# A third pair of q-k products added on VectorE, background steps counted by their pitch, late softmaxes kept in PSUM, and a later load of T2

## The chip, the cores and the metric

The kernel runs on one core of one Trainium2 chip. The metric is the device time of one launch in microseconds (us); 715.28 is the median of three runs before the change.

## The reference

```python
x = A_x                                               # (1, 2048, 1024) bf16
g = _sigmoid((x * gate_w).sum(-1, keepdims=True))
# A: local attention, 32 heads of 32, 8 keys at distances 0, 2, ..., 14 behind the query
qkv = (x @ wqkv).reshape(B, S, 3, H, Dh) ...
logits = jnp.einsum("bhsd,bhswd->bhsw", q, kg) * Dh ** -0.5
logits = jnp.where(mask[None, None, :, :], logits, -1e9)
attn = _softmax(logits, axis=-1)
a = einsum("bhsw,bhswd->bhsd", attn, vg) ... @ wo
# B: gated MLP, Dm = 1024, Df = 3584
b = (_gelu(x @ w_gate) * (x @ w_up)) @ w_down
out = g * a + (1 - g) * b
```

## The kernel before

All large products are done by a seven-product scheme for 2 x 2 blocks: sums and differences of blocks ("forms") are made by VectorE, seven products by TensorE, and the results are put together in PSUM by copies and additions.

**The loop of units.** `units` lists 78 units: a pair of MLP columns, 16 units of q and k (eight for each half `s` of the sequence), eight of v, then the other MLP pairs, a gate and an up unit each. Iteration `b` is called a slot here. In each slot TensorE does, in this order, p1 of unit b (4 matmuls), p73 of unit b-1 (8), p5 of unit b (4), p2 and p6 of unit b (8), p4 of unit b-1 (4): 28 matmuls of 512 columns, all on line 355. The addition at the end of p73 (L401) is VectorE's: it reads the banks Y and Z, and p4 writes Y again. ScalarE copies banks (L377, L382, L390) and evacuates results (L361, L363, L409).

**Background tasks.** What VectorE does besides L401 comes from generators that stand in `tasks`, ordered by a priority. `run_bg(b, period)` is called once at the end of each slot: the credit is at most 0.3 left over plus the period (4.7 us in q, k and v, 4.8 after), and while it is over 0.3, the first task that is awake does a step and its price, a number that the step yields, is taken off. All of this happens while the program is recorded; on the chip the order is fixed. `Task.finish()` does all remaining steps of a task at once. The tasks that matter here:

- `sums_pair` (L315): four sums of weights for each MLP pair.
- `h_task` (L246, for the last pairs also L249): h = gelu(gate) * up, then a store to `h_d` on POOL's DMA queue (L252).
- `qk_prods` (L603 for two tiles at a time, L596 for one): the products q * k for 8 keys and three blocks of 256 positions each; each tile of 2048 columns stands in one of six buffers `prod`. `reduce_mm` on TensorE (L608) sums over head dimensions into banks 5 to 7: 12 matmuls for the products of one unit. For the units in `ADDED`, `qk_add` (L641) first adds the products of two units, and one reduction serves both.
- `spill` (L603, L596, L679 to L686): the same for the fourth block of each half, from q and k stored before.
- `softmax` and `softmax_back`: maximum (L713), subtraction (L715), exponential on ScalarE (L723), sum (L730), reciprocal, gate, product (L735), and a store to `w_d`. `softmax(a, cnt, ...)` does `cnt` blocks from block `a` on; number `e` says which of five it is. The exponent's argument and result stand in the arena (SBUF), at `R_EX[e]`.
- `pv_all` (L772 multiplies, L778 folds): attention times v for eight blocks, four tiles at a time, then a store to `o_d` (L796).
- `t_forms` (L895, L898), forms of the output weights, stored to `t_d`.

**The seam.** `run_last` follows the loop. It does p73 and p4 of the last unit, starts `down(0)`, queues the loads of T1 and T2 on SP's DMA queue and finishes all tasks. `pre_down_2` and `pre_down_3`, called when PV is done, have loaded most of the operands A12, A21, A22 and R21 (L838, L840, L857, on SP); `pre_down_4` queues the last parts of the four A operands on POOL's queue (L838): these come from `h_d` and wait for the last pair's first h store. `down(s)` then computes the output rows of half `s`: products of 512 columns (L1104) and, in `level2`, of 256 columns (L1071, seven products of 18 matmuls a group), with forms by VectorE: L943 scales, L952 combines, `forms_L` (L1029) and `forms_R` (L1037).

Of the kernel before, what the change touches and what calls it, by code (L numbers as in the profile page):

```python
# [15 lines left out]
P = 128  # L16
SC = 512
# [19 lines left out]
R_EX = (194.5, 81, 50, 81, 84)  # L37
R_MD = 72
R_ATTN = 73
# [3 lines left out]
R_PROD = 84  # L43
# [25 lines left out]
def kernel(  # L69
# [68 lines left out]
    with tc.manual_schedule(engines={mybir.EngineType.PE, mybir.EngineType.DVE, mybir.EngineType.Activation,  # L138
# [145 lines left out]
        def gate_task(s):  # L284
            ts = slice(s * SUP, (s + 1) * SUP)
            zc = small.tile([P, HK, ZI], F32, tag="zc", bufs=2)
            zs = small.tile([P, ZI], F32, tag="zs", bufs=2)
            go = small.tile([P, 2, ZI], BF16, tag="go", bufs=2)
            yield None
            nc.gpsimd.dma_start(out=zc[:], in_=z_d[:, ts].rearrange("g (p i) -> p g i", i=ZI))  # L290
            yield None
            V.tensor_reduce(out=zs[:], in_=zc[:].rearrange("p g i -> p i g"), axis=AX.X, op=ALU.add)
            nc.scalar.activation(out=zs[:], in_=zs[:], func=ACT.Tanh, scale=0.5)
            yield 0.15
            yield None
# [12 lines left out]
            gated.add(s)  # L308

        def sums_pair(w, sm):  # L310
            L11, L12 = w[:, :, 0:HK, 0:P], w[:, :, HK:KT, 0:P]
            L21, L22 = w[:, :, 0:HK, P:2 * P], w[:, :, HK:KT, P:2 * P]
            for o_, a, b_, op in ((sm[:, 0], L21, L22, ALU.add), (sm[:, 1], sm[:, 0], L11, ALU.subtract),
                                  (sm[:, 2], L11, L21, ALU.subtract), (sm[:, 3], L12, sm[:, 1], ALU.subtract)):
                TT(out=o_, in0=a, in1=b_, op=op)  # L315
                yield 0.64
# [97 lines left out]
        now = [0]  # L414

        class Task:
# [11 lines left out]
            def finish(self):  # L428
                while not self.done:
                    self.step()  # L430
# [7 lines left out]
        credit = [0.0]  # L438
# [54 lines left out]
        def h_task(G, U, i, s):  # L493
            h_store(G, U, i, s)
            yield 1.14 if i < NSC else 2.3

        def add_gu(w, sm, i, s):
            ug = add_unit(gu_forms(w, sm, 0), xf[s], "gate", st_tile)
            uu = add_unit(gu_forms(w, sm, 1), xf[s], "up", st_tile)
            uu.fin = lambda: bg(h_task(ug.T, uu.T, i, s), *((5.5, now[0]) if (i, s) == (NPAIR - 1, 0) else (7.5 if i == NPAIR - 1 else 0, now[0] + 1)))  # L500
# [74 lines left out]
        pr_off = [R_PR, R_PR + 4, R_PROD, R_PR + 8, R_PR + 12, R_PROD + 4]  # L575
# [19 lines left out]
        def qk_mult(dst, q, k):  # L595
            TT(out=dst, in0=q.rearrange("p (o s) -> p o s", o=1).to_broadcast([P, NWIN, AC]),  # L596
               in1=_win_ap(k, [[-DIL, NWIN], [1, AC]]), op=ALU.mult)

# [3 lines left out]
        def qk_mult2(dst, q, k, sq, sk):  # L602
            TT(out=dst, in0=_win_ap(q, [[sq, 2], [0, NWIN], [1, AC]]),  # L603
               in1=_win_ap(k, [[sk, 2], [-DIL, NWIN], [1, AC]]), op=ALU.mult)
# [7 lines left out]
        ADDED = {(1, 1), (1, 7)}  # L612
# [3 lines left out]
        def qk_prods(u, s, t):  # L616
# [21 lines left out]
        def qk_add(s, t):  # L638
            for a, b in ((0, 3), (2, 5)):
                u, v = ((pair_at(pr_off[i], pr_off[i + 1]) if a == 0 else reg(pr_off[i], NWIN * AC)) for i in (a, b))  # L640
                TT(out=u, in0=u, in1=v, op=ALU.add)  # L641
                yield 2.21 if a == 0 else 1.14
# [18 lines left out]
        SPILL = ((((R_PR, R_PR + 4), (R_PR + 8, R_PR + 12)), ((R_PR + 8, R_PR + 12), (R_PROD, R_PROD + 4))),  # L661
                 (((R_PROD, R_PROD + 4), (R_PR + 4, R_PR + 12)), ((R_PR + 4, R_PR + 12), (R_PR, R_PR + 8))))

        def spill(s):
# [3 lines left out]
            for g, (x, y) in enumerate(SPILL[s]):  # L668
                for i, ef in enumerate((x, y)):
                    t = QG * g + 2 * i  # L670
                    if credit[0] > 1.5:
                        qk_mult2(pair_at(*ef), qb[s][:, t, :], kb[s][:, t, HALO:HALO + AC], AC, KV)
                        yield 2.21
                        continue
                    for j in range(2):
                        qk_mult(reg3(ef[j], NWIN, AC), qb[s][:, t + j, :], kb[s][:, t + j, HALO:HALO + AC])
# [24 lines left out]
        def softmax(a, cnt, b0, e):  # L701
            ee = regf(R_EX[e], cnt * SC)
            e4 = ee.rearrange("p (a w s) -> p a w s", a=cnt, w=NWIN)
            sw = ee.rearrange("p (a w s) -> p a s w", a=cnt, w=NWIN)
            lg = banks[:, b0:b0 + cnt, :]
# [8 lines left out]
            yield 0.55 * cnt + 0.05  # L714
            TT(out=e4, in0=src, in1=bc(m), op=ALU.subtract)  # L715
            yield 0.55 * cnt + 0.05
# [5 lines left out]
        def softmax_exp(a, cnt, ee, e4, sw, m, bc):  # L722
            nc.scalar.activation(out=ee, in_=ee, func=ACT.Exp, scale=scale)  # L723
            bg(softmax_back(a, cnt, ee, e4, sw, m, bc), 3, now[0] + 1)

        def softmax_back(a, cnt, ee, e4, sw, m, bc):
# [7 lines left out]
            yield 0.65 * cnt  # L734
            TT(out=attn_all[:, a:a + cnt, :].rearrange("p a (w s) -> p a w s", w=NWIN), in0=e4, in1=bc(d), op=ALU.mult)  # L735
            yield 0.55 * cnt + 0.05
# [17 lines left out]
        def pv_all():  # L754
# [5 lines left out]
            for i, a in enumerate(PVO):  # L760
# [19 lines left out]
                for t in range(0, NT, 4):  # L780
                    if i + 1 == NBLK and t == 4:
                        load_A(Bs(0)["A12"], 0, 1, 0, 0, KX, False)
                    for step, n_ in ((lambda u, m: mult(u, m), 2), (lambda u, m: fold(u, m, 4), 4)):
                        u = t
                        while u < t + 4:
# [4 lines left out]
                            yield 2.21 if m == n_ else 1.14  # L790
                    fold(t, 4, 2)
                    yield 1.14
# [27 lines left out]
        at(Q0 + 2 * NT, lambda: [sv_task.step() for _ in range(2 - sv_n[0])])  # L820
        due(Q0 + 2 * NT + 1, sv_task)
# [45 lines left out]
        def load_T(b, k):  # L867
            nc.sync.dma_start(out=b, in_=t_d[k - 1][:])
# [18 lines left out]
        def t_forms():  # L887
            for q in range(NQ):
# [7 lines left out]
                yield 1.14  # L896
                for o_, a, b_ in ((r22, r22, r11), (r21, r21, r22)):
# [4 lines left out]
                    yield 0.61  # L902
# [356 lines left out]
        def run_last(b):  # L1259
# [8 lines left out]
            loads(0, "T1", "T2")  # L1268
            for t_ in list(tasks):
                t_.finish()  # L1270
            run(first)
            run(down(1))

        def head():
            xs, f = xf[0], []
            for i, o in enumerate((R_PROD, R_ATTN)):
# [65 lines left out]
        for b in range(Q0, n):  # L1342
# [22 lines left out]
            run_bg(b, (4.7 if b < NQKV else 4.8) + extra)  # L1365
# [34 lines left out]
```

## Time and profile before

| | |
|---|---|
| median of three runs | 715.28 us (715.12 to 715.37) |
| the profiled execution | 715.41 us |
| its span, first to last instruction | 713.6 us |
| TensorE's granted clock | 0.999 |
| DMA | 162.03 MB, 227 GB/s |

In rows of instructions stand line, engine, operation, output and input, count, then busy time, mean ns of one, and the idle time before them with what ended it. In the chain that ended last and in the timeline a row stands for a run of like instructions: start, length, what, count. In rows of windows stand the length, then PE, PEld, DVE, ACT and POOL busy with counts, the granted clock, the DMA share and GB/s. PE is TensorE, DVE VectorE, ACT ScalarE, POOL GpSimd. Instructions on VectorE overlap at their ends, so the time from start to start, called pitch, is shorter than the duration.

### The profile page before, as it was taken

Reading aid. Unit: us, or ns where it says so; the run is one execution under the profiler, and the core shown is the slowest. Engines: PE = TensorE matmul, PEld = TensorE weight load, DVE = VectorE, ACT = ScalarE, POOL = GpSimd, SP = SyncE. Lnnn points to the kernel's source line nnn. Section 1 sums busy time; section 2 is a strip of 40 time slices with the busy share of each in tenths; the row PEclk is TensorE's granted clock in tenths of the full one; section 3 lists DMA queues with packets and bytes.
Section 4 is the critical chain, followed back from the end, with each engine's and each line's share of the span. In section 5 each row is a group of like instructions: output and inputs, shape, how many; then the busy total and the mean of one; then the engine's idle time right before and its main releaser. Section 6 shows DMA issues by size and latency. Waiting matters only on the chain.

```text
span 713.6 us, 10641 instructions
## 1 busy us (share of the span) xinstructions
PE 704.6 (99%) x4021; PEld 407.4 (57%) x4077; DVE 675.4 (95%) x641; ACT 329.8 (46%) x602; POOL 143.6 (20%) x248
## 2 busy tenths in 40 slices
PE   9999999999999999999999999999999999999998
PEld 4466666655544444444444444444447886758887
DVE  3999999999999999999999999999789999899997
ACT  5554445445557665555555555555322321132431
POOL 1243444115502432221210100101110002100011
PEclk9999999999999999999999999999999999999999
DMA  9989454283375768575662764372981799995951
GB/s 296 326 227 274 153 183 151 85 216 126 118 244 186 234 200 270 163 242 180 216 181 95 273 209 164 114 269 64 393 347 39 305 402 400 421 427 219 386 227 60
DMA packets 94755, 162.03 MB, mean 227 GB/s; under 512 B 23680, under 2 KB 71200, under 8 KB 90352
## 3 DMA queue, kind: packets, MB, share of 16 engines
q1 hardware_dynamic: 77632, 105.46, 43.0%
q0 software_dynamic: 16352, 48.29, 20.0%
q10 hardware_dynamic: 720, 7.60, 2.7%
q8 instruction: 32, 0.52, 0.3%
q14 instruction: 19, 0.16, 0.1%
HBM read 112.17 MB, written 54.14 MB: 233 GB/s over the span
## 4 chain that ended last, share of the span: by engine, by line
PE 96%; DVE 2%; DMA 1%; issue 1%; SPq 0%; ACT 0%; DVEq 0%
PE banks L355 67%; PE banks L1071 19%; PE banks L1104 9%; PE banks L608 2%; DMA arena<-in_B_w_gate_dram 1%; DVE arena L401 0%; DVE arena L943 0%; PE banks L274 0%; DVE arena L772 0%; DVE arena L1285 0%; DVE arena L246 0%; DVE arena L249 0%; DVE arena L223 0%; SPq L144 0%; ACT arena L363 0%
## 5 line engine op out<-in xcount | busy, mean ns | idle before, releaser
L355 PE MATMUL banks<-arena 128*128 128x512 bf16 x2191 | 484.7, 379 | 4.2 <-DVE arena L401 0.9
L355 PEld LDWEIGHTS <-arena 128*128 128x128 bf16 x2240 | 245.7, 110 | 241.4 <-issue 7.7
L1071 PE MATMUL banks<-arena 128*128 128x256 bf16 x1260 | 138.3, 273 | 0.0
L1071 PEld LDWEIGHTS <-arena 128*128 128x128 bf16 x1260 | 123.3, 98 | 15.2 <-issue 0.3
L382 ACT COPY arena<-banks 128x512 f32<-128x512 f32 x80 | 46.9, 586 | 129.7 <-PE banks L355 129.7
L401 DVE TENSOR_TENSOR arena<-banks,arena 128x1024 bf16<-128x1024 f32 x80 | 97.4, 1219 | 4.7 <-PE banks L355 4.0
L363 ACT CAST arena<-banks 128x512 bf16<-128x512 f32 x104 | 60.8, 585 | 42.4 <-PE banks L355 41.1
L772 DVE TENSOR_TENSOR arena<-arena 128x2048 bf16<-128x2048 bf16 (+1 forms) x45 | 74.1, 1670 | 0.4
L778 DVE TENSOR_TENSOR arena<-arena 128x2048 bf16<-128x2048 bf16 (+2 forms) x54 | 68.1, 1261 | 1.0
L252 POOL DMA_DIRECT2D h_d<-arena x28 | 20.3, 730 | 232.8 <-DVE arena L246 154.5
L1104 PE MATMUL banks<-arena 128*128 128x512 bf16 x281 | 62.4, 379 | 0.4
L390 ACT COPY banks<-banks 128x512 f32<-128x512 f32 x80 | 45.6, 570 | 22.3 <-PE banks L355 20.7
L1029 DVE TENSOR_TENSOR arena<-arena 128x2304 bf16<-128x2304 bf16 x40 | 53.3, 1353 | 0.5
L377 ACT COPY banks<-banks 128x512 f32<-128x512 f32 x80 | 46.1, 576 | 14.4 <-PE banks L355 13.3
L1076 ACT COPY banks<-banks 128x256 f32<-128x256 f32 x60 | 21.4, 356 | 59.7 <-PE banks L1071 59.5
L603 DVE TENSOR_TENSOR arena<-arena 128x4096 bf16<-128x4096 bf16 x21 | 47.9, 2284 | 0.3 <-ACT arena L382 0.2
L1104 PEld LDWEIGHTS <-arena 128*128 128x128 bf16 x288 | 28.2, 98 | 33.5
L952 DVE TENSOR_TENSOR arena<-arena 128x2048 bf16<-128x2048 bf16 (+1 forms) x40 | 41.8, 1113 | 3.4 <-DMA arena<-h_d 3.4
L361 ACT ACTIVATE arena<-banks 128x512 bf16<-128x512 f32 x56 | 33.4, 597 | 20.8 <-PE banks L355 20.7
L1037 DVE TENSOR_TENSOR arena<-arena 128x2304 bf16<-128x2304 bf16 x28 | 37.7, 1353 | 0.2
L315 DVE TENSOR_TENSOR arena<-arena 128x1024 bf16<-128x1024 bf16 x56 | 36.1, 686 | 0.5
L246 DVE TENSOR_TENSOR arena<-arena 128x2048 bf16<-128x2048 bf16 x28 | 34.0, 1216 | 2.5 <-ACT arena L363 2.5
(99 smaller groups left out, 459.2 us busy)
## 6 DMA issues: line engine op xcount, KB each, us to landing
arena<-t_d SPq DMA_DIRECT2D x8, 2304.0 KB, 13.4
h_d<-arena POOLq DMA_DIRECT2D x28, 512.0 KB, 4.3
arena<-w_c SPq DMA_DIRECT2D x12, 1152.0 KB, 14.1
t_d<-arena POOLq DMA_DIRECT2D x36, 256.0 KB, 4.4
arena<-h_d SPq DMA_DIRECT2D x6, 1536.0 KB, 12.6
arena<-in_B_w_down_dram SPq DMA_DIRECT2D x28, 256.0 KB, 6.2
r_d<-arena ACTq DMA_DIRECT2D x3, 2304.0 KB, 9.6
arena<-r_d SPq DMA_DIRECT2D x3, 2304.0 KB, 14.3
```

The costliest lines, as they stand in the source:

```text
L355: self.pe = nc.tensor.matmul(ps, lhsT=self.L[form](kt), rhs=rhs[:, kt, :], start=(start and kt == 0), stop=(kt == HK - 1), skip_group_chec ...
L363: nc.scalar.copy(out=o_, in_=i_)
L377: nc.scalar.copy(out=self.Y, in_=self.X)
L382: nc.scalar.copy(out=self.p5s, in_=self.V)
L390: nc.scalar.copy(out=self.Z, in_=self.Y)
L401: TT(out=self.T[:, :, c2s], in0=pair, in1=self.p5s.rearrange("p (o n) -> p o n", o=1).to_broadcast([P, 2, SC]), op=ALU.add)
L603: TT(out=dst, in0=_win_ap(q, [[sq, 2], [0, NWIN], [1, AC]]), in1=_win_ap(k, [[sk, 2], [-DIL, NWIN], [1, AC]]), op=ALU.mult)
L772: TT(out=prod2[:, t % 4:t % 4 + m, :], in0=flat(ab).rearrange("p (o n) -> p o n", o=1).to_broadcast([P, m, NWIN * AC]), in1=_win_ap(v[:, t ...
L778: TT(out=h(0) if w > 1 else o_[:, t:t + m, :], in0=h(0), in1=h(1), op=ALU.add)
L1029: TT(out=o_, in0=a, in1=b_, op=op)
L1071: nc.tensor.matmul(c(i, h, j), lhsT=l[:, kt, j * P:(j + 1) * P], rhs=r[:, kt, :], start=False, stop=(kt == KH - 1), skip_group_check=True)
L1104: nc.tensor.matmul(ps, lhsT=L[:, i, j * P:(j + 1) * P], rhs=R[:, i, :], start=(start and q == 0), stop=(q == NK - 1), skip_group_check=not ...
```

## The change

- Products of the q-k units 4 and 5 of the second half are added too (`ADDED` has a third entry). One instruction now does up to three tiles, in the products and in the additions; how many is decided by the credit. The six buffers lie side by side.
- The prices that background steps yield are set to the measured pitches, and the credit per slot is 4.8 in q, k and v, and 4.85 after. Steps done by `finish()` are taken off the credit as well.
- Softmaxes 2 to 4 (the three blocks of the second half, and the two spill blocks) write the exponent's argument and result in place, in the banks in PSUM. Their regions in the arena are dropped, and others move.
- The second half of the first softmax is not awake before the slot after the q-k units.
- The h task of the last MLP pair's first half has priority 6.5 instead of 5.5. The gate task yields once more before its first sum. Two steps of `sums_v` are due one slot earlier.
- The load of T2 goes to POOL's queue and stands behind all remaining tasks.

```diff
-R_EX = (194.5, 81, 50, 81, 84)
-R_MD = 72
-R_ATTN = 73
+R_EX = (88, 81)
+R_MD = 80
+R_ATTN = 84
...
             nc.gpsimd.dma_start(out=zc[:], in_=z_d[:, ts].rearrange("g (p i) -> p g i", i=ZI))
             yield None
+            yield None
...
-                    self.step()
+                    credit[0] -= self.step() or 0.0
...
-            uu.fin = ... ((5.5, now[0]) if (i, s) == (NPAIR - 1, 0) else ...
+            uu.fin = ... ((6.5, now[0]) if (i, s) == (NPAIR - 1, 0) else ...
...
-        pr_off = [R_PR, R_PR + 4, R_PROD, R_PR + 8, R_PR + 12, R_PROD + 4]
+        pr_off = [R_PR + 4 * k for k in range(6)]
...
+        def run_at(o, m):
+            return reg(o, m * NWIN * AC)
+        COST = {1: 1.14, 2: 2.21, 3: 3.28}
+        def steps(m):
+            return min(m, 1 + (credit[0] > 1.5) + (credit[0] > 2.6))
+        def qk_mult(dst, q, k, m, sq, sk):
+            TT(out=dst, in0=_win_ap(q, [[sq, m], [0, NWIN], [1, AC]]),
+               in1=_win_ap(k, [[sk, m], [-DIL, NWIN], [1, AC]]), op=ALU.mult)
...
-        ADDED = {(1, 1), (1, 7)}
+        ADDED = {(1, 1), (1, 5), (1, 7)}
...
             while a < ND:
-                if a == 0 and credit[0] > 1.5:
-                    qk_mult2(pair_at(pr_off[k], pr_off[k + 1]), u.T[:, 0, 0:AC], u.T[:, 1, 0:AC], AC, AC)
-                    a += 2
-                    yield 2.21
-                else:
-                    qk_mult(out_[a], u.T[:, 0, a * AC:(a + 1) * AC], u.T[:, 1, a * AC:(a + 1) * AC])
-                    a += 1
-                    yield 1.14
+                m = steps(ND - a)
+                qk_mult(run_at(pr_off[k + a], m), u.T[:, 0, a * AC:(a + m) * AC], u.T[:, 1, a * AC:(a + m) * AC], m, AC, AC)
+                a += m
+                yield COST[m]
...
-            ee = regf(R_EX[e], cnt * SC)
+            lg = banks[:, b0:b0 + cnt, :]
+            ee = regf(R_EX[e], cnt * SC) if e < 2 else lg.rearrange("p a n -> p (a n)")
...
-            bg(softmax_back(a, cnt, ee, e4, sw, m, bc), 3, now[0] + 1)
+            bg(softmax_back(a, cnt, ee, e4, sw, m, bc), 3, max(now[0] + 1, (Q0 + 2 * NT + 1) * (a == 0)))
...
-            yield 0.9 * cnt + 0.05
+            yield 0.54 * cnt + 0.18 if a > BPS - 2 else 0.93 * cnt + 0.13
...
-                            yield 2.21 if m == n_ else 1.14
+                            yield (2.21 if m == n_ else 1.14) + 0.11 * (n_ == 4 and u == t + 4)
                     fold(t, 4, 2)
-                    yield 1.14
+                    yield 1.26
...
-            loads(0, "T1", "T2")
+            loads(0, "T1")
             for t_ in list(tasks):
                 t_.finish()
+            load_T(Bs(0)["T2"], 2, nc.gpsimd)
...
-            run_bg(b, (4.7 if b < NQKV else 4.8) + extra)
+            run_bg(b, (4.8 if b < NQKV else 4.85) + extra)
```

More of the change, by code (lines that the diff above doesn't have):

```diff
@@ L414 @@
         now = [0]
+        credit = [0.0]
         class Task:
@@ L436, in bg @@
             return t
-        credit = [0.0]
         def run_bg(b, period):
@@ L544, in sums_v @@
                 sv_n[0] += 1
[L545 removed]
+                yield 1.25 if sv_n[0] < 3 else 1.14
         def v_forms(t):
@@ L638, in qk_add @@
         def qk_add(s, t):
-            for a, b in ((0, 3), (2, 5)):
-                u, v = ((pair_at(pr_off[i], pr_off[i + 1]) if a == 0 else reg(pr_off[i], NWIN * AC)) for i in (a, b))
+            a = 0
+            while a < ND:
+                m = steps(ND - a)
+                u, v = (run_at(pr_off[a + b], m) for b in (0, ND))
                 TT(out=u, in0=u, in1=v, op=ALU.add)
-                yield 2.21 if a == 0 else 1.14
+                a += m
+                yield COST[m]
             slotq.append((0.8, lambda: qk_reduce(s, t - 1, prods[t - 1], 2)))
@@ L819 @@
         sv_task = bg(sums_v(), 2.1, TFE + 2)
-        at(Q0 + 2 * NT, lambda: [sv_task.step() for _ in range(2 - sv_n[0])])
-        due(Q0 + 2 * NT + 1, sv_task)
+        at(Q0 + 2 * NT - 1, lambda: [sv_task.step() for _ in range(2 - sv_n[0])])
+        due(Q0 + 2 * NT, sv_task)
         for s in range(2):
@@ L865, with load_T @@
                 at(NQKV + 10 + 6 * m_ + e_, lambda k_=k_, i_=i_: lay_out(k_, i_))
-        def load_T(b, k):
-            nc.sync.dma_start(out=b, in_=t_d[k - 1][:])
+        def load_T(b, k, eng=nc.sync):
+            eng.dma_start(out=b, in_=t_d[k - 1][:])
         NP = 2
@@ L1275, in head @@
             xs, f = xf[0], []
-            for i, o in enumerate((R_PROD, R_ATTN)):
+            for i, o in enumerate((R_PR + 16, R_ATTN)):
                 for m in range(2):
```

37 lines of the change are left out of this document (15 added, 22 removed).

## The prediction

> **What bounds the kernel now.** I read the page first, then windows of 100 us, the chain that ended last, VectorE's timeline, and last the DMA view of the stage where the loop hands over to the output products.
>
> ```profile
> span 713.6 us, 10641 instructions
> PE 704.6 (99%) x4021; PEld 407.4 (57%) x4077; DVE 675.4 (95%) x641; ACT 329.8 (46%) x602; POOL 143.6 (20%) x248
> 300.00:400.00 100.00, 99.53 (x455) 45.17 (x462) 99.06 (x86) 55.87 (x92) 18.86 (x26) 1.00 0.62 194
> 363.11 10.74 PE banks L355 x49
> 122.18 0.76 PE banks L608 x12
> 148.84 1.41 PE banks L608 x24
> ```
>
> TensorE is busy 99% at full clock (the 1.00 in the window row), and the chain's usual piece is 49 matmuls in 10.74 us. One matmul lasts 0.379 us (10.74 less 48 pitches), so the pitch is 0.216 us, and a slot of the loop, 28 matmuls, takes 6.05. VectorE is busy 99% too: per slot it has one L401 for TensorE and whatever background steps the credit lets through. So there are three ways to gain: fewer matmuls, fewer waits of TensorE for L401, and shorter waits at the seams.
>
> TensorE's waits in the loop are small and hang on L401, the addition that frees the two banks which p4 writes next. Between p73's last matmul and p4's first stand p5, p2 and p6: 12 matmuls, 2.59 us. Less L401 itself (1.22) and the last result's 0.2 to 0.3, L401 may start some 1.1 us late before p4 waits.
>
> ```profile
> 114.95 2.75 PE banks L355 x12
> 117.71 4.48 PE banks L355 x20
> 253.62 4.54 PE L355 MATMUL banks<-arena 128*128 128x512 bf16 x18
> 373.90 10.88 PE banks L355 x49
> 395.62 10.83 PE banks L355 x49
> 471.26 10.88 PE banks L355 x49
> 506.54 2.82 PE L355 MATMUL banks<-arena 128*128 128x512 bf16 x12 [0.89 <-DVE arena L401]
> ```
>
> From 114.95 to 117.71 are 2.76 us for 12 matmuls, 0.17 too many. The row at 253.62 has 18 matmuls and one record missing (the records drop about one matmul in 50); 19 should take 4.27, so 0.27 is lost. The three pieces of 49 are 0.14, 0.09 and 0.14 over 10.74. Together 0.8. The row at 506.54 is the big one: 0.89 idle after the last end is 0.89 + 0.379 - 0.216 = 1.05 us of lost pitch.
>
> **The change, part by part.** *Third added pair.* The products of tiles 4 and 5 of the second half are added by VectorE and reduced once. The x24 row is a pair reduced without adding, the x12 row one with: TensorE gains 1.41 - 0.76 = 0.65 us, all on the path.
>
> ```profile
> L603 DVE TENSOR_TENSOR arena<-arena 128x4096 bf16<-128x4096 bf16 x21 | 47.9, 2284 | 0.3 <-ACT arena L382 0.2
> L596 DVE TENSOR_TENSOR arena<-arena 128x2048 bf16<-128x2048 bf16 x22 | 26.6, 1218 | 0.0
> L730 DVE TENSOR_REDUCE arena<-arena 128x192 f32<-128x1536 f32 x1 | 2.8, 2841 | 0.0
> L713 DVE TENSOR_REDUCE arena<-banks 128x192 f32<-128x1536 f32 x1 | 1.8, 1757 | 0.4 <-PE banks L608 0.4
> L730 DVE TENSOR_REDUCE md<-arena 128x64 f32<-128x512 f32 x3 | 3.1, 1027 | 0.0
> L713 DVE TENSOR_REDUCE md<-banks 128x64 f32<-128x512 f32 x3 | 2.1, 686 | 0.1
> ```
>
> VectorE pays for the addition. 4096 columns cost 1.07 more than 2048, so 6144 take 3.35, about 3.27 start to start. The same form now does three tiles at once: in the changed order 13 triples are one instruction instead of two (2.20 + 1.13 start to start), 0.06 less each, 0.8. The late softmaxes stay in PSUM: the sum over 1536 columns should cost what the maximum from PSUM costs, 1757 instead of 2841 ns, and the two of 512 columns 686 instead of 1027: 1.08 + 0.68 = 1.8 less. The other rows of a softmax have the same columns and element type whatever the source. The trace has no sum from PSUM and no exponential in PSUM; the bounds are no gain at all (1027 per 512) and the maximum's price, and I take the latter, being the same instruction on the same source. Net: 3.3 - 0.8 - 1.8 = 0.7 us more on VectorE.
>
> [...]
>
> *Steps counted by pitch, credit 4.85.*
>
> ```profile
> 299.71 2.28 DVE L772 TENSOR_TENSOR arena<-arena 128x4096 bf16<-128x4096 bf16 x1
> 302.03 2.29 DVE L778 TENSOR_TENSOR arena<-arena 128x4096 bf16<-128x4096 bf16 x1
> 304.24 1.22 DVE L401 TENSOR_TENSOR arena<-banks,arena 128x1024 bf16<-128x1024 f32 x1
> 305.37 2.61 DVE L315 TENSOR_TENSOR arena<-arena 128x1024 bf16<-128x1024 bf16 x4
> 307.90 1.95 DVE L778 TENSOR_TENSOR arena<-arena 128x2048 bf16<-128x2048 bf16 x2
> 309.76 1.22 DVE L401 TENSOR_TENSOR arena<-banks,arena 128x1024 bf16<-128x1024 f32 x1
> 310.90 1.22 DVE L246 TENSOR_TENSOR arena<-arena 128x2048 bf16<-128x2048 bf16 x1
> ```
>
> Start to start, a multiplication followed by its fold takes 2.32 (299.71 to 302.03), the fold 2.21, the last two folds 1.86, and L401 1.13. Four tiles of PV are two multiplications and the folds: 2.21 + 2.32 + 2.21 + 1.86 = 8.60. The old count is 2.21 x 3 + 1.14 + 0.61 = 8.38, the new one 2.21 x 2 + 2.32 + 1.26 + 0.61 = 8.61. So the old credit of 4.8 let 4.8 x 8.60 / 8.38 = 4.93 through, with L401 6.06 per slot against TensorE's 6.05: a lag is never worked off, and steps of 2.2 push it over the 1.1 again and again. The new 4.85 lets 4.84 through, 5.97 per slot. I followed the changed order slot by slot with these pitches. Its heaviest stretch comes before PV: L401, four L315 and spill's additions of 4096 and 2048 columns, 1.13 + 2.53 + 2.21 + 1.14 = 7.01 in a slot of 6.05, so the next L401 is 0.96 late; after a slot of 5.56 the lag is 0.48, and one of 7.16 in 6.64 (a reduction makes it longer) leaves 1.0. From there to the end it stays under 0.9. I therefore take the 0.8 as removed and put 0.15 back for lags a little above my pitches. The time per slot that is no longer used is found at the end, where the old order left the last slot empty.
>
> *The seam.*
>
> ```profile
> 496.38 0.80 SPq L838 DMA_DIRECT2D arena<-h_d  x2
> 497.40 1.22 DVE L401 TENSOR_TENSOR arena<-banks,arena 128x1024 bf16<-128x1024 f32 x1
> 501.13 1.23 DVE L246 TENSOR_TENSOR arena<-arena 128x2048 bf16<-128x2048 bf16 x1 [2.51 <-ACT arena L363]
> 504.14 0.72 POOL L252 DMA_DIRECT2D h_d<-arena  x1 [6.27 <-issue]
> 505.27 1.22 DVE L401 TENSOR_TENSOR arena<-banks,arena 128x1024 bf16<-128x1024 f32 x1
> 512.23 2.17 POOL L838 DMA_DIRECT2D arena<-h_d  x4 [7.36 <-DMA h_d<-arena]
> 513.52 27.79 PE L1104 MATMUL banks<-arena 128*128 128x512 bf16 x125
> 531.27 1.29 DVE L952 TENSOR_TENSOR arena<-arena 128x1024 bf16<-128x1024 bf16 x2 [3.36 <-DMA arena<-h_d]
> 541.31 55.17 PE banks L1071 x504
> 574.76 1.35 DVE L1037 TENSOR_TENSOR arena<-arena 128x2304 bf16<-128x2304 bf16 x1
> q1 hardware_dynamic: 275, 4.42, 74.9%
> q0 software_dynamic: 403, 1.35, 24.2%
> ```
>
> The last pair's first h task (priority 5.5, woken in its own slot) makes VectorE wait 2.51 us for a value that ScalarE has just been given, L401 queues behind it, and TensorE loses the 1.05. At priority 6.5 the task stands one slot later, behind ready scaling steps: in the changed order the last slot reads L401, two L943, L246, L249, 5.3 us of work in 6.05. The 1.05 goes. That step's store and what waits on it move too, and the cover must be named: the store L252 releases POOL's four loads L838, and VectorE's longest wait of this stage, 3.36 us up to 531.27, is for them. From there VectorE runs without a pause to beyond 576.11, the end of the L1037 at 574.76. TensorE needs that result in the fifth product of the third group, 2 x 126 + 72 = 324 matmuls of 55.17 / 504 = 0.1095 us after about 541.2: at 576.6. So whatever TensorE has gained by then, it keeps only as far as the loads land earlier, plus 0.5.
>
> When they land: PV's last steps now fall into the slot of 497.40, so SP's loads of 496.38, which need its buffers, start some 4.4 later. The due time of the L401 at 505.27 was 497.40 + 6.05 = 503.45; with 1.4 gained by then (0.65 and the small stalls) 502.1, and after two L943 (1.13 as L246, and 0.60 for half the columns), L246 and L249 the store goes out near 507.7 instead of 504.14. It took 8.1 to release the loads (512.23), beside SP's loads; lightly loaded, h stores land in 4.3 (median, below), so 512.0 to 515.8. The four loads took 19.0, because SP's T1 and T2 filled the engines: POOL's queue had 24.2% of their time against 74.9% in the DMA rows (518 to 532).
>
> ```profile
> h_d<-arena POOLq DMA_DIRECT2D x28, 512.0 KB, 4.3
> DMA to landing us min/median/max: 9.7/17.0/19.4
> ```
>
> T2 is now queued on POOL behind these loads. The landing row is that of the three loads of T issued between 480 and 560; T1's is the 17.0, from 509.4 to 526.4; with SP 4.4 later but one h store fewer beside it (0.5 MB, 1.3 us at the 5.77 MB in 14 us of both queues), 529.5, SP's queue is empty and the rest of the loads, about a fifth at the old rate from 513.9, comes within a microsecond. So 526 (POOL at its 1.35 MB in 14 us throughout) to 533 (the old 19.0 from 513.9); I take 529.5, the nearest to the rows with SP's queue shortened: 1.8 earlier than 531.27. T2 itself is read by VectorE after 550 and can take 15 us on POOL's queue at no cost.
>
> *The rest.* The first softmax's second half moves behind the q-k stage, and the gate's first sum one slot back; both stay within slots that have room and cost nothing. The products' buffers change places: the one at 64 KB is still read by the stores of t_d, which are issued one slot ahead of the first use; nothing.
>
> **Sum.** TensorE: 0.65 + 0.8 - 0.15 + 1.05 = 2.35. VectorE's cap: 1.8 + 0.5 = 2.3. They nearly meet; I take 2.2. The profiled execution took 715.41 (span 713.6 and 1.8 around it), 0.13 over the median of 715.28: 713.2 against the profiled one, 713.1 against the median. A measurement of this kernel can tell about 0.2%, 1.4 us, from no change.
>
> **Rivals.** *The gain is given back at 576.* The loads land at 530.5 to 531.5, so the cap is 1.2 to 0.2: 714.1 to 715.1. For it: the store leaves 3.6 later. Against: T2's 2.3 MB no longer stand beside the loads. Chance 0.20.
>
> *Slower.* The four loads keep their old distance from the store, 531.27 - 504.14 = 27.1, and land at 534.8. The first is A11's last part, which TensorE needs 48 matmuls after 513.5, at 523.9, less the gain; VectorE's unbroken run then ends 3.5 late, TensorE loses 3.0 net: 718.3. It decides against the change by over 0.2% from a landing after 533.2. For it: SP's queue also starts 4.4 later, so it may overlap the loads as long as before. Chance 0.12.
>
> [...] Chance 0.05.
>
> *The budget does not do what it says*: steps of 3.3 us make L401 as late as before, and the 0.8 stays: 713.1 + 0.65 = 713.8. For it: new single steps are longer than any before. Against: they sit where a reduction widens the tolerance by 0.8 to 1.9. Chance 0.06.
>
> The forecast has 0.57. Faster by over 0.2% means under 713.85: the forecast and some two thirds of the last two, 0.64. Within: 0.20 + 0.04 = 0.24. Slower 0.12. Low end: nothing put back and no cap, 2.65, and 0.2 for the rest: 712.4. High end 715.8, which takes in the first rival and the near part of the second. The forecast's own range is 712.5 to 713.8.
>
> **What would show it.** Right: L608 rows fall by 12; chain pieces of 49 at 10.74 throughout from 360 to 480; no wait of TensorE for L401 near 505; reductions of 1536 columns from PSUM at 1.76 in both places; VectorE's wait for arena<-h_d ends near 529.5 or before. Wrong: a TensorE wait for L1037 or its line's successor near 576, or one on arena<-h_d near 522; pieces over 10.74 with L401 as releaser.

## The result and the profile after

| | us | ratio to before, 95% interval |
|---|---|---|
| before, median of six runs beside it | 715.19 | |
| after, median of six runs (717.98 to 722.81) | 718.62 | 1.0058 [1.0037, 1.0079] |
| after, a second series (717.95 to 723.21) | 719.28 | 1.0061 [1.0041, 1.0081] |
| forecast | 713.1 (712.4 to 715.8) | |

The change makes the kernel slower by about 3.4 to 4 us. The forecast was faster; what came is the rival called *Slower* (718.3), which had a chance of 0.12. The profiled execution of after took 722.81 us (span 720.3); it is the slowest of its six, and has two early waits that are separated from the rest below.

First the page of after and its windows in the loop, against the rows of before at the head of the prediction. A window's row has its length, then PE, PEld, DVE, ACT and POOL busy, and the granted clock.

```profile
span 720.3 us, 10652 instructions
PE 709.7 (99%) x4065; PEld 407.5 (57%) x4065; DVE 676.4 (94%) x626; ACT 330.2 (46%) x602; POOL 144.3 (20%) x249
PEclk9999999999999999999999999999989999999999
```

```profile
300.00:400.00 100.00, 100.00 (x465) 45.30 (x463) 98.64 (x86) 55.91 (x93) 18.08 (x25) 1.00 0.59 183
400.00:500.00 100.00, 100.00 (x465) 45.35 (x464) 98.83 (x84) 55.06 (x92) 8.33 (x11) 1.00 0.53 180
```

The loop did become what the forecast said, but these rows alone don't show it. The trace of before lacks some ten matmul records in the window from 300 to 400 (x455 for x465), and each leaves a gap of 2 x 0.216 - 0.379 = 0.05 us, which is about all that its 99.53 leaves open. A stall under 0.379 - 0.216 = 0.16 us doesn't show in busy time at all. What shows the gain is the pitch in the chain of waits (start, length, what, count). In before the stretch from 355 to 485 holds stalls of 0.14, 0.09 and 0.14; in after it is one piece of 604 matmuls, 603 pitches of 0.2156:

```profile
354.85 130.36 PE banks L355 x604
```

But the clock's row has an 8 near the end, which before does not have. The rows of TensorE's waits (line, what it waited for, us in total, times, longest) show what is new:

```profile
PE banks L1109 <- DMA arena<-h_d: 4.0, 1, 4.0
PE banks L355 <- DVE arena L401: 2.2, 2, 1.1
```

The first is the seam. Its timeline in after, where a row is start, length, engine, line, what, count and the idle time before it:

```profile
504.48 1.22 DVE L401 TENSOR_TENSOR arena<-banks,arena 128x1024 bf16<-128x1024 f32 x1
505.62 1.81 DVE L948 TENSOR_TENSOR arena<-arena,omgrep 128x2048 bf16<-128x2048 bf16 x2
507.35 1.22 DVE L245 TENSOR_TENSOR arena<-arena 128x2048 bf16<-128x2048 bf16 x1
508.60 1.22 DVE L248 TENSOR_TENSOR arena<-arena,omgrep 128x2048 bf16<-128x2048 bf16 x1
510.35 0.72 POOL L251 DMA_DIRECT2D h_d<-arena  x1 [5.77 <-issue]
513.54 10.52 PE L1109 MATMUL banks<-arena 128*128 128x512 bf16 x48
519.23 2.16 POOL L843 DMA_DIRECT2D arena<-h_d  x4 [8.16 <-DMA h_d<-arena]
528.04 8.31 PE L1109 MATMUL banks<-arena 128*128 128x512 bf16 x24 [3.98 <-DMA arena<-h_d]
532.66 1.29 DVE L957 TENSOR_TENSOR arena<-arena 128x1024 bf16<-128x1024 bf16 x2 [4.48 <-DMA arena<-h_d]
```

The order on VectorE is the one forecast (L401, two L948, L245, L248), and the wait for L401 near 505 is gone. The store L251 goes out at 510.35. POOL's loads, which wait for it, are issued at 519.23, and TensorE has done its 48 matmuls by 523.9 and stands still until the first load has landed. Then 24 matmuls take 8.31 us instead of 5.3: the first 14 of them run at half clock, as the windows say.

```profile
522.00:525.00 3.00, 2.06 (x10) 0.74 (x8) 3.00 (x4) 0.00 (x0) 0.66 (x2) 1.00 1.03 434
525.00:528.00 3.00, 0.00 (x0) 0.00 (x0) 3.00 (x3) 0.00 (x0) 0.00 (x0) 0.87 1.00 421
528.00:531.00 3.00, 2.96 (x7) 1.03 (x8) 0.18 (x1) 1.35 (x3) 0.00 (x0) 0.50 0.97 381
531.00:534.00 3.00, 3.00 (x9) 1.07 (x8) 1.34 (x3) 2.01 (x4) 0.00 (x0) 0.50 1.09 459
534.00:537.00 3.00, 3.00 (x15) 1.41 (x14) 3.00 (x3) 0.17 (x1) 0.00 (x0) 0.99 0.99 424
```

So the seam costs the wait, 3.98 + 0.16 = 4.1 us of lost pitch, and 14 matmuls at a pitch of 0.427 instead of 0.216, 2.9 us.

The second row of waits, 2.2 us for L401, is near 63 and 70. It begins with the transposed load of x, on which VectorE stands still:

```profile
62.31 1.23 DVE L207 TENSOR_TENSOR arena<-arena 128x2048 bf16<-128x2048 bf16 x1 [3.02 <-DMA arena<-in_A_x_dram]
64.72 6.20 PE L355 MATMUL banks<-arena 128*128 128x512 bf16 x28 [1.08 <-DVE arena L401]
```

This is the part that the first experiments had to tell from the seam.

### The profile page after: what moved, and what is told of

Read it like the earlier page. It is cut to its first block, busy times and chain, and to the rows that moved or that the text cites. A ratio compares the mean times of both kernels' runs of the same rounds, so it can differ in the third digit from the quotient of the medians.

```text
span 720.3 us, 10652 instructions
## 1 busy us (share of the span) xinstructions
PE 709.7 (99%) x4065; PEld 407.5 (57%) x4065; DVE 676.4 (94%) x626; ACT 330.2 (46%) x602; POOL 144.3 (20%) x249
## 4 chain that ended last, share of the span: by engine, by line
PE 93%; DVE 2%; issue 2%; DMA 2%; ACT 0%; POOL 0%; SPq 0%; DVEq 0%; POOLq 0%
PE banks L355 65%; PE banks L1076 19%; PE banks L1109 7%; PE banks L612 1%; DMA arena<-h_d 1%; DMA arena<-in_A_x_dram 1%; DVE arena L783 1%; DVE arena L401 1%; DVE arena L607 0%; PE banks L273 0%; DVE arena L1291 0%; DVE arena L222 0%; DVE arena L207 0%; PE banks L218 0%; DVE arena L948 0%
## 5 line engine op out<-in xcount | busy, mean ns | idle before, releaser
L355 PE MATMUL banks<-arena 128*128 128x512 bf16 x2240 | 487.5, 379 | 2.7 <-DVE arena L401 2.2
L355 PEld LDWEIGHTS <-arena 128*128 128x128 bf16 x2240 | 245.8, 110 | 242.1 <-issue 8.0
L401 DVE TENSOR_TENSOR arena<-banks,arena 128x1024 bf16<-128x1024 f32 x80 | 97.4, 1218 | 4.1 <-PE banks L355 2.2
L777 DVE TENSOR_TENSOR arena<-arena 128x4096 bf16<-128x4096 bf16 (+1 forms) x39 | 73.6, 1902 | 0.3
L607 DVE TENSOR_TENSOR arena<-arena 128x6144 bf16<-128x6144 bf16 (+2 forms) x30 | 72.2, 2425 | 0.8 <-PE banks L612 0.8
L1109 PE MATMUL banks<-arena 128*128 128x512 bf16 x288 | 65.9, 391 | 4.0 <-DMA arena<-h_d 4.0
L251 POOL DMA_DIRECT2D h_d<-arena x28 | 20.4, 733 | 227.4 <-DVE arena L245 144.7
L1081 ACT COPY banks<-banks 128x256 f32<-128x256 f32 x60 | 21.4, 356 | 59.5 <-PE banks L1076 59.3
L957 DVE TENSOR_TENSOR arena<-arena 128x2048 bf16<-128x2048 bf16 (+1 forms) x40 | 41.8, 1110 | 4.5 <-DMA arena<-h_d 4.5
L1042 DVE TENSOR_TENSOR arena<-arena 128x2304 bf16<-128x2304 bf16 x28 | 37.6, 1350 | 0.7 <-DMA arena<-t_d 0.5
L245 DVE TENSOR_TENSOR arena<-arena 128x2048 bf16<-128x2048 bf16 x28 | 33.9, 1214 | 0.0
## 6 DMA issues: line engine op xcount, KB each, us to landing
h_d<-arena POOLq DMA_DIRECT2D x28, 512.0 KB, 4.3
```

The costliest lines, as they stand in the source:

```text
L355: self.pe = nc.tensor.matmul(ps, lhsT=self.L[form](kt), rhs=rhs[:, kt, :], start=(start and kt == 0), stop=(kt == HK - 1), skip_group_chec ...
L401: TT(out=self.T[:, :, c2s], in0=pair, in1=self.p5s.rearrange("p (o n) -> p o n", o=1).to_broadcast([P, 2, SC]), op=ALU.add)
L607: TT(out=dst, in0=_win_ap(q, [[sq, m], [0, NWIN], [1, AC]]), in1=_win_ap(k, [[sk, m], [-DIL, NWIN], [1, AC]]), op=ALU.mult)
L777: TT(out=prod2[:, t % 4:t % 4 + m, :], in0=flat(ab).rearrange("p (o n) -> p o n", o=1).to_broadcast([P, m, NWIN * AC]), in1=_win_ap(v[:, t ...
L1109: nc.tensor.matmul(ps, lhsT=L[:, i, j * P:(j + 1) * P], rhs=R[:, i, :], start=(start and q == 0), stop=(q == NK - 1), skip_group_check=not ...
```

## The experiments

Two theories. *Seam*: the last pair's h store goes out later relative to TensorE's need of the first of POOL's four loads, TensorE waits, and its clock falls. *Early*: the change's shifts in the first slots let L207 meet x too soon, and L401 is late near 63 and 70.

**late_xforms** lets the forms of x for the second half (L207) wake two slots later.

```diff
-        due(Q0 + NT, bg(late_forms(), 3, Q0 + 3))
+        due(Q0 + NT, bg(late_forms(), 3, Q0 + 5))
```

> The changed kernel with one edit: the sums of x for the second half wake two slots later, so that they do not stand ahead of their transposed loads. Theory 1 (the changed kernel loses 2.5 us at two TensorE waits near 63 and 71 us, because these sums, now a slot earlier, hold VectorE 3.0 us for x): no such waits, about 2.5 us less than the changed kernel's 718.6, so 716.1; the wait for h near 524 us stays. Rival (the transposed loads were late by chance in the profiled execution alone, 62.1 us against 58.2 before): no change, 718.6, and the whole loss sits near 524.

719.55 us, 1.0059 [1.0047, 1.0072]. The early waits are absent, the seam's wait is there (4.68 of idle), and the time is that of after. So the early waits are not what makes the kernel slower, though the edit has a price of its own.

```profile
118.10 4.26 PE L355 MATMUL banks<-arena 128*128 128x512 bf16 x19 [0.77 <-DVE arena L401]
508.51 0.72 POOL L251 DMA_DIRECT2D h_d<-arena  x1 [5.78 <-issue]
518.21 2.16 POOL L843 DMA_DIRECT2D arena<-h_d  x4 [8.98 <-DMA h_d<-arena]
526.89 3.39 PE L1109 MATMUL banks<-arena 128*128 128x512 bf16 x8 [4.68 <-DMA arena<-h_d]
```

The first of these rows is new: the work that was put off makes L401 late near 117 instead, 0.93 us of pitch.

**prio55** undoes the h task's priority alone.

```diff
-... (6.5, now[0]) if (i, s) == (NPAIR - 1, 0) else ...
+... (5.5, now[0]) if (i, s) == (NPAIR - 1, 0) else ...
```

> The changed kernel with the h task of the last pair's first half back at priority 5.5. In the built order its store then stands in the last slot but one, right behind PV's last folds, some 4.3 us earlier than in the changed kernel (510.4 there). Theory 1 (TensorE waits 4.1 us for the last part of A11, which that store releases, and then runs 13 matmuls at half pitch): the wait near 524 shrinks to under 0.5 us and the slow matmuls go; 3 to 6 us less than 718.6, 712.6 to 715.6. Rival (SP's loads, which start 7 us later because PV ends a slot later, are what delays the last part): the wait stays over 2.5 us, 717 or more.

713.19 us, 0.9973 [0.9962, 0.9983]: faster than both kernels, and what the forecast's sum says, although the gain of 1.05 is not the way it was to come. The store is back at 504.03 and the first load is in time; TensorE runs through, at full clock throughout the execution (mean 1.0).

```profile
503.42 1.22 DVE L401 TENSOR_TENSOR arena<-banks,arena 128x1024 bf16<-128x1024 f32 x1
504.03 0.72 POOL L251 DMA_DIRECT2D h_d<-arena  x1 [1.77 <-ACT arena L382]
504.69 2.75 PE L355 MATMUL banks<-arena 128*128 128x512 bf16 x12 [0.22 <-DVE arena L401]
511.60 23.69 PE L1109 MATMUL banks<-arena 128*128 128x512 bf16 x109
513.52 2.16 POOL L843 DMA_DIRECT2D arena<-h_d  x4 [8.76 <-DMA h_d<-arena]
529.81 1.29 DVE L957 TENSOR_TENSOR arena<-arena 128x1024 bf16<-128x1024 bf16 x2 [3.82 <-DMA arena<-h_d]
```

At priority 5.5 the wait for L401 that cost 1.05 costs 0.38 here (0.22 + 0.379 - 0.216), because the rest of the change has moved VectorE's work. The priority saves that 0.38 and on the whole costs 5.4 to 6.1 us (718.62 and 719.28 against 713.19).

**late_xforms_prio55** has both edits.

> Both edits together. If both losses are real and independent: 718.6 - 2.5 - 3.4 = 712.7, faster than before (715.2) by the prediction's own sum for TensorE, 2.35. If the early wait was chance, the same as with the priority alone. If VectorE's later stages take it back near 576 (the prediction's cap), 714 to 715.

714.12 us, 0.9985 [0.9976, 0.9994]: 0.9 above prio55, the price of the late forms as seen at 117 (0.92 here).

**before_prio65** makes the priority the one edit to before.

```diff
-... (5.5, now[0]) if (i, s) == (NPAIR - 1, 0) else ...
+... (6.5, now[0]) if (i, s) == (NPAIR - 1, 0) else ...
```

> The kernel before with the priority 6.5 as its one edit. In its built order PV still ends a slot earlier, so the store moves by under 1 us: VectorE does the scaling steps while it waits for ScalarE. Theory 1 (the priority alone is good, and only together with PV's later end does it delay the store): the 1.05 us wait for L401 near 505 goes and no wait for h appears, 714.2 to 714.5. Rival (priority 6.5 by itself delays the loads): a wait near 524, 716 or more.

714.88 us, 0.9992 [0.9983, 1.0001]: alone it is not told from no change. In the old order PV ends a slot earlier (SP's loads, which wait for it, start at 496.38 instead of 503.46), and the store goes out at 504.91, 0.8 later than in before; its loads are in time for the products. The 1.05 at 505 goes, and in the profiled execution (the slowest of the eleven) 1.27 comes back where the prediction put its cap: VectorE's wait for the last of the loads ends at 532.70, and TensorE meets L1037 in the fifth product of the third group.

```profile
504.91 0.72 POOL L252 DMA_DIRECT2D h_d<-arena  x1 [6.28 <-issue]
514.03 2.17 POOL L838 DMA_DIRECT2D arena<-h_d  x4 [8.40 <-DMA h_d<-arena]
532.70 1.29 DVE L952 TENSOR_TENSOR arena<-arena 128x1024 bf16<-128x1024 bf16 x2 [5.15 <-DMA arena<-h_d]
577.59 2.58 PE L1071 MATMUL banks<-arena 128*128 128x256 bf16 x22 [1.11 <-DVE arena L1037]
```

So the priority costs over 5 us in one order and nothing that can be told in the other. The prediction saw what joins them (PV's later end and so SP's later loads) but priced it for the last of the four loads alone.

**prio55_next_slot** keeps the delay and drops the queueing: priority 5.5, awake one slot later.

```diff
-... (6.5, now[0]) if (i, s) == (NPAIR - 1, 0) else ...
+... (5.5, now[0] + 1) if (i, s) == (NPAIR - 1, 0) else ...
```

> The changed kernel with the last pair's first h task at priority 5.5 but woken one slot later (the old change of priority is undone, the delay to the next slot kept, without standing behind the scaling steps). In the order of VectorE its store then stands about 1.8 us ahead of where the changed kernel has it: near 508.5 instead of 510.35. Theory (TensorE waits for the first of the four loads, and the store's place sets it): the wait of TensorE on arena<-h_d in front of the 48th to 49th matmul of the first group shrinks by about 1.8 us, to 2.0 to 2.5, and the time is between 714.9 and 717, with part of the gain again from a shorter or absent stretch at half clock. Rival (the loads are slow because T1 and R21 of SP compete, whatever the store's place): the first load still lands near 527 to 528, the wait stays near 4, the time near 718.6.

713.41 us, 0.9976 [0.9968, 0.9985]: neither case came. The store goes out at 506.33, not 508.5, and there is no wait at all, at the seam or for L401.

```profile
506.33 0.72 POOL L251 DMA_DIRECT2D h_d<-arena  x1 [4.03 <-ACT arena L361]
511.26 24.12 PE L1109 MATMUL banks<-arena 128*128 128x512 bf16 x111
513.89 2.16 POOL L843 DMA_DIRECT2D arena<-h_d  x4 [6.83 <-DMA h_d<-arena]
```

A store 2.3 later than in prio55 releases the loads only 0.4 later (513.89 against 513.52). So the step from store to release isn't a constant: 9.5 us in prio55, 7.6 here.

**after_t1_on_pool** keeps priority 6.5 and puts T1's load behind the four loads on POOL's queue.

```diff
-            loads(0, "T1")
...
+            load_T(Bs(0)["T1"], 1, nc.gpsimd)
             load_T(Bs(0)["T2"], 2, nc.gpsimd)
```

> The changed kernel, priority 6.5 kept, with T1's load too put on POOL's queue behind the four late loads: SP's queue has then only the loads of raw blocks beside them. It asks how much of the seam's loss is contention and how much the store's place. Theory (place): store unchanged at 510.4, the h store lands somewhat sooner (4.3 to 6 us instead of 8.6) and the first load within 3 to 5 us of its issue instead of 8.8, so it lands at 518 to 522, TensorE's wait goes or falls under 0.5 and the time is 713 to 714.5. Rival (T1 is not what competes, it is R21 and the other loads of SP): first load at 526 to 528, time 717.5 to 719. T1 landing later may cost up to 1 us where its sums are read.

713.83 us, 0.9981 [0.9973, 0.999]. The store still takes as long to release the loads, but the first load then lands 5.3 us after its issue instead of 8.8, and TensorE loses 0.76 instead of 4.1, with no drop of the clock (mean 1.000).

```profile
509.55 0.72 POOL L251 DMA_DIRECT2D h_d<-arena  x1 [5.77 <-issue]
512.74 10.52 PE L1109 MATMUL banks<-arena 128*128 128x512 bf16 x48
518.48 2.17 POOL L843 DMA_DIRECT2D arena<-h_d  x4 [8.20 <-DMA h_d<-arena]
523.87 11.40 PE L1109 MATMUL banks<-arena 128*128 128x512 bf16 x52 [0.60 <-DMA arena<-h_d]
```

So the loss needs both: a late store, and T1 beside the loads that it releases. Either remedy brings the time back. That T1 alone makes a load slow doesn't follow: with the store earlier, the first load takes 6.7 us without T1 (next_slot_t1_on_pool, below) and 6.9 with it (prio55_next_slot).

**prio55_t2_on_sp** undoes "T2 loads later" on top of prio55.

```diff
-            loads(0, "T1")
+            loads(0, "T1", "T2")
...
-            load_T(Bs(0)["T2"], 2, nc.gpsimd)
```

> The changed kernel with priority 5.5 as before the change, and T2's load on SP's queue behind T1's as before the change: it isolates 'T2 loads later'. Theory of the prediction (SP's T1 and T2 slow POOL's four loads; VectorE's run from the last of them to the result of L1042 is what TensorE meets in the middle of the products): the last of the four loads lands 1.5 to 3 us later than the 529.7 of the same kernel with T2 on POOL, VectorE has no slack left, TensorE waits 1 to 2 us for L1042 near 576, time 714.2 to 715.2. Rival (the loads go at their own rate): last load at 529.7, time 713.2, no wait near 576.

714.16 us, 0.9982 [0.9973, 0.999]. VectorE's wait for the last load ends at 530.34 instead of 529.81, 0.5 later and not 1.5 to 3, and near 576 TensorE has 0.38 of idle time for L1042. So moving T2 helped by little, some 0.5 us in the trace (0.38 + 0.379 - 0.216 there, no stall in prio55). Whether it is worth the whole 1 us between the two medians, which come from different series, the intervals don't tell.

**before_added** makes the third pair the one edit to before.

```diff
-        ADDED = {(1, 1), (1, 7)}
+        ADDED = {(1, 1), (1, 5), (1, 7)}
```

> The kernel before with (1, 5) put into the set of added pairs as its one edit. The prediction's term: TensorE runs 12 matmuls fewer, 0.65 us; VectorE gets 3.3 us more to do under the old credit of 4.8 that already let 4.93 per slot through. Theory of the prediction: the 0.65 is gained ahead of the last slots but VectorE's cap (four loads, then its unbroken run to the result of L1037) takes it back, and later L401s may cost it again: 714.7 to 715.5, not told from before by more than 0.3. Rival (no cap, matmuls count in full): 714.65, with no wait near 576.

719.97 us, 1.0058 [1.0046, 1.007]: a miss by 5 us. VectorE's 3.3 us more don't fit the old plan. The sums of the v weights (L543) are due at the end of the q-k stage; pushed back, they come up against the next L355 that needs them:

```profile
147.49 1.22 DVE L543 TENSOR_TENSOR arena<-arena 128x2048 bf16<-128x2048 bf16 x1
148.77 4.50 PE L355 MATMUL banks<-arena 128*128 128x512 bf16 x12 [2.75 <-DVE arena L543]
```

```profile
147.00:150.00 3.00, 1.23 (x4) 0.56 (x5) 1.71 (x2) 0.00 (x0) 0.00 (x0) 0.82 0.99 364
150.00:153.00 3.00, 3.00 (x10) 1.11 (x8) 0.59 (x1) 0.00 (x0) 0.00 (x0) 0.61 1.31 236
```

2.9 us are lost there, some 1.7 more in a stretch at half clock behind it, and 1.09 near 580 for L1037. The changed kernel has none of these waits, so its other edits together give the pair its room. Which of them does (three tiles a step, sums in PSUM, the first softmax's second half or the v sums moved) was not tried.

**after_again** is after itself, beside the next three.

> The changed kernel as it is, in the same series as its variants. Theory (TensorE's wait for the first of POOL's four loads, then a stretch at half clock): 718 to 719, a wait on arena<-h_d of 3.5 to 4.5 us about 10.5 us after the products begin, mean granted clock 0.995 to 0.998 in every execution, and none of the two early waits of 1.25 and 1.30 us near 63 and 70 that the first profiled execution had. Rival (the early waits belong to the kernel): they stand again at 63 and 70.

719.28 us, a little above the range. The seam's wait is 3.35, the clock 0.50 behind it, and the mean clock 0.995 to 0.998 in each of the six executions, where prio55's ran at 0.999 or 1.000. The early waits stand in the profiled execution again (0.78 near 63 and 1.29 near 70): the theory that they were of one execution falls. Four of the nine traces whose forms of x stand as in after have them (after twice, and both with T1 on POOL, of which after_t1_on_pool has only the second), always with L207 waiting 1.9 to 3.0 for x, and each of the four was the slowest or second slowest execution of its kernel, 1.4 to 4.2 us over the median. That they weigh little in the medians is likely but not shown.

The changed order lets these waits in. In before the second of these forms starts at 64.51, and x has landed by 58.16. In the changed order VectorE is ready for it a slot earlier, near 59.3. The last part of x lands at 56.5 to 59.7 in the other five traces, and at 61.3 to 62.1 in these four. So here too a step was moved up to the landing of a load; why x lands late in these four was not tried and stays open.

**next_slot_old_budget** undoes the pitches and credits on top of prio55_next_slot; three of the places are shown.

```diff
-                yield 1.25 if sv_n[0] < 3 else 1.14
+                yield 1.14
...
-                    yield 1.26
+                    yield 1.14
...
-            run_bg(b, (4.8 if b < NQKV else 4.85) + extra)
+            run_bg(b, (4.7 if b < NQKV else 4.8) + extra)
```

> prio55_next_slot with the old counts of the steps (1.14 for 1.25 and 1.26, 0.64, 2.3, 0.61 for 0.73) and the old credits of 4.7 and 4.8 per slot; the counts of the three-tile steps and of the softmaxes stay new. It undoes 'steps counted by their pitch'. Theory of the prediction: the old credit lets some 4.9 through where 4.84 fits, L401 comes too late in single slots, and TensorE loses 0.4 to 0.8 in waits of 0.1 to 0.4: 713.8 to 714.2. Rival (the small waits came from the order before and not from the count): 713.3 to 713.5.

713.73 us, 0.9985 [0.9975, 0.9994], against 0.9976 for the new count. The trace has loop waits of 0.06, 0.17, 0.34 and 0.12, together 0.69, where prio55_next_slot has 0.10: some 0.6 us, near the 0.8 less 0.15 of the sum. The ratios to before agree in sign and size, but their intervals overlap, so the 0.6 rests on the traces.

**next_slot_four_added** adds a fourth pair.

```diff
-        ADDED = {(1, 1), (1, 5), (1, 7)}
+        ADDED = {(1, 1), (1, 3), (1, 5), (1, 7)}
```

> prio55_next_slot with (1, 3) in the set of added pairs too: a fourth pair. TensorE runs 12 matmuls fewer, 0.65. If VectorE has room for 3.3 us more: 712.8. If it hasn't (theory: its slots are full, as the run with a third pair and the old plan showed): in the order of its instructions one slot of the second half of the q-k stage holds about 8.8 us of work against TensorE's 6.05, L401 comes 1.5 to 2 us too late there, TensorE waits 0.5 to 2 us near 118 to 124, and the last slot holds some 8 us: 714 to 716.

721.37 us, 1.0077 [1.0065, 1.0089], over 5 us above the range. VectorE has no room for it: TensorE loses 2.67 near 143, 1.2 near 513 and 2.24 at the seam, where the store is late again (510.63).

```profile
146.25 4.04 PE L355 MATMUL banks<-arena 128*128 128x512 bf16 x17 [2.51 <-DVE arena L401]
527.62 2.82 PE L1109 MATMUL banks<-arena 128*128 128x512 bf16 x7 [2.07 <-DMA arena<-h_d]
```

```profile
147.00:150.00 3.00, 3.00 (x16) 1.81 (x15) 3.00 (x4) 1.16 (x2) 0.56 (x2) 1.00 0.31 78
528.00:531.00 3.00, 3.00 (x9) 1.03 (x7) 3.00 (x3) 1.85 (x4) 0.00 (x0) 0.50 1.02 429
```

**next_slot_t1_on_pool** joins the two remedies.

> prio55_next_slot with T1's load on POOL's queue behind the four late loads, as in after_t1_on_pool. prio55_next_slot has no wait at the seam, and 0.48 us left where TensorE meets L1042 near 574. Theory (the last of the four loads is held back by T1 and sets that): the last load lands 3 to 4 us sooner, the 0.48 goes, 712.8 to 713.1. Rival: T1 now lands later than VectorE wants it (near 532), its sums wait 2 to 4 us and the gain is gone or reversed: 713.4 to 714.5.

712.99 us, 0.9970 [0.9960, 0.9980], the fastest median here, though not told apart from prio55 or prio55_next_slot. The last load lands at 526.4 instead of 529.9, and the stall near 576 falls from 0.48 to 0.2 at most; VectorE's sums then wait 3.7 us for T, but no wait of TensorE follows from that.

## Why the prediction was wrong, step by step

*The third pair*: right in size. The group of L612 has 172 rows for 184, and its chain pieces are 12 matmuls in 0.76. That it is "all on the path" needs the change's other edits: in before_added, without them, VectorE's added work costs more than the matmuls save.

*VectorE's costs*: right.

```profile
L607 DVE TENSOR_TENSOR arena<-arena 128x6144 bf16<-128x6144 bf16 x13 | 43.5, 3350 | 0.8 <-PE banks L612 0.8
L734 DVE TENSOR_REDUCE arena<-banks 128x192 f32<-128x1536 f32 x1 | 1.7, 1745 | 0.0
L734 DVE TENSOR_REDUCE md<-banks 128x64 f32<-128x512 f32 x2 | 1.4, 683 | 0.0
```

Three tiles take 3.35 as worked out, and the sums read from PSUM cost what the maximum costs: 1745 for 2841 ns, and 683 for 1027. For these sums over a strided view the read from PSUM is the cheaper one, by 0.34 us at 512 columns and 1.1 at 1536; the difference grows with the columns, some 0.7 ns for each. The chance of 0.05 is for sums that gain nothing from PSUM: no run shows that, and the rows of after show 1745 and 683 ns in its place.

*Pitches and credit*: right. In before L401's pitch is shorter than its duration (1.13 us for 1.22), but that of a multiplication of PV ahead of its fold is not (2.32 for 2.28). The loop has no stall from 355 to 485, and undoing them brings 0.6 us of waits back in the trace.

*The seam* is the step that failed, and not in its first half. The store's place was forecast well: 507.7 with TensorE 2.45 ahead of before (its 1.4 and the 1.05) puts it 13.75 us ahead of the need at 523.9 - 2.45 = 521.45; measured are 523.9 - 510.35 = 13.55. The second half priced the moved store by the *last* of the four loads and VectorE's cap at 576, and gave the *first* load, which TensorE needs 48 matmuls into the products, no landing time; only the rival names its need, and it puts no price on it. The landing of the first load (us at the end of each row) in before, after and after_t1_on_pool:

```profile
arena<-h_d POOLq DMA_DIRECT2D x1, 256.0 KB, 7.5
arena<-h_d POOLq DMA_DIRECT2D x1, 256.0 KB, 8.8
arena<-h_d POOLq DMA_DIRECT2D x1, 256.0 KB, 5.3
```

What the runs show in place of the failed step, with "needed" as the start of the 48 matmuls plus 48 pitches of 0.216:

| | store out | loads issued | first load lands | needed | in hand |
|---|---|---|---|---|---|
| before | 504.14 | 512.23 | 519.71 | 523.88 | 4.2 |
| before_prio65 | 504.91 | 514.03 | 522.87 | 523.53 | 0.7 |
| prio55 | 504.03 | 513.52 | 520.35 | 521.96 | 1.6 |
| prio55_next_slot | 506.33 | 513.89 | 520.84 | 521.62 | 0.8 |
| after_t1_on_pool | 509.55 | 518.48 | 523.82 | 523.10 | -0.7 |
| after | 510.35 | 519.23 | 528.00 | 523.90 | -4.1 |

The cover was 4.2 us, and it was in the trace of before. The forecast moved the store 6 us closer to the need and hoped for 0 to 4 of it back in a shorter release (512.0 to 515.8, that is 4.3 to 8.1 after the store). Its own upper end with the 7.5 that the first load took in before is 523.3, 1.8 us after the need: the wait stood inside the forecast's own bounds. Then both terms came out above them. The release took 8.9, with SP's loads, which also start later, beside the store, as the rival says for itself; the 4.3 was the median of all 28 h stores, while the two ahead of this need took 9.2 and 7.5 in before. And the first load took 8.8 with T1 beside it; 5.3 with T1 out of the way.

*The rival's price* was nearly right by luck. Its 3.0 us is the last load again: landing at 534.8, 3.5 late, less the 0.5 of slack that VectorE's run has at 576. Measured, VectorE's wait for the last load ends at 532.66, 22.3 after the store and not 27.1, and TensorE has no wait at 576. It lost its time at the first load, which landed 17.7 after the store against 15.6 in before: 3.5 to 4.1 in the two traces of after, and 2.9 of half clock behind that. These two executions have a mean clock of 0.995; most of the others have 0.998, so their slow stretch was shorter. With the 7 or 8 slow matmuls of other runs it costs about 1.6, an estimate, and prio55's 713.2 + 3.5 to 4.1 + 1.6 = 718.3 to 718.9, against medians of 718.62 and 719.28.

*The cap at 576* exists (before_prio65: 1.27 us there), and T2 on POOL loosens it by 0.5 and not by most of 1.8. In after it doesn't show, since TensorE comes there late.

*"The rest"* was not tried by itself. prio55 meets the forecast's sum without a charge for it. But the changed order of the first slots has the early waits, and which of the edits moved L207 was not tried. *The budget* did what it says.

## What to carry to other kernels

When a step that others wait for is moved, list every reader of what it releases and set the earliest need first: here four loads left in one row, and the argument followed the last of them while the first had 4.2 us in hand for a move of 6. Give a transfer that is moved into a busier stretch the row of its nearest neighbour in that stretch (7.5 to 9 us), not the median over the kernel (4.3). Price an idle time of a few us of TensorE above its length (here 2.2 us brought some 1.6 more and 4.1 us 2.9 more, though 2.7 us brought none), and keep a step's priority apart from its time: awake one slot later is not the same as behind everything that is ready.

## What the hardware showed

A short idle time of TensorE can cost more than itself. Behind 4.1 us of lost time (after) and 3.5 (after_again) 14 matmuls ran at a pitch of 0.427 instead of 0.216; behind 4.8 (late_xforms), 2.9 (before_added) and 2.2 (next_slot_four_added, at the seam) some 7 or 8; behind 2.7 (next_slot_four_added, near 143) and all of 1.3 and less, none. So the 2.2 cost more than the 2.7.

In the slow stretches the granted clock was 0.50 (after, 528 to 534; next_slot_four_added, 528 to 531), and they took some 3 or 6 us. The length of the idle time alone does not decide in these runs; what does was not shown.
